# Reordering one DMA queue inside a software-pipelined attention, and the warm-up transposes ahead of it

## The chip, the cores and the metric

The kernel runs on one core of a Trainium2 chip. The metric is device time in microseconds (us); less is better. TensorE (PE) does the matmuls and the transposes, VectorE (DVE) and ScalarE (ACT) the elementwise work and the reductions, GpSimd (POOL) some more of it, and SyncE (SP) issues nearly all DMAs, one after another from one queue: what stands at its head and waits holds up all behind it.

## The reference

```python
q_n, k_n = rmsnorm(q, g_q), rmsnorm(k, g_k)          # q, k, v: 4 x 12 heads x 448 x 64, float32
scores = matmul(q_n, k_n.T) / sqrt(64)
attn = softmax(scores)                               # divided by (its row sum + 1e-9)
x = matmul(attn, v)                                  # rearranged to 1792 x 768
x = ((x @ w_a) * (x @ w_b)) @ w_out                  # 768 -> 1536 -> 768
x = (sigmoid(x @ w_gate) * (x @ w_val)) @ w_out2
```

The change concerns the attention alone.

## The kernel before

The attention works on 24 pairs of heads, one pair on the two halves of the 128 partitions. It is software-pipelined by hand. Three lists say what is emitted and in which order: `begin` (a prologue), then `turns` once for each pair (`first` is the turn of the second pair), then `end`. An entry such as `(put, -2)` calls `put` for the pair two before that of the turn. Nothing reorders the emitted instructions: the lists set the order on every engine, and that of SP's queue.

What a pair goes through, spread over several turns:

- `load`, `load_r`, `load_v`: SP loads Q, K, the remaining 64 rows, and V. The buffers are few, so each load waits for the last reader of what stood there.
- `squares`, `mean`, `rsqrt`, `newton`, `scale`: the rms normalization, the last on GpSimd. `t_tr` transposes Q and K on TensorE, `k_hi`, `k_lo`, `q_hi`, `q_lo` split each in a high and a low part.
- `s`: scores, three matmuls for each block of rows, in one of three PSUM banks (`ps_s`). `top` and `exp` take the row maximum (DVE) and the exponential with its row sum (ACT).
- `x_tr`, `x_out`: transposes of the exponentials in a unit (`unit()`, one of two two-bank PSUM tiles that all transposes share) and copies out of it. `pv`: matmuls with V, all four blocks of a pair into one PSUM bank, `pvs`, of which there is one.
- `rsum` (reciprocals of the row sums), `rsum_tr`, and `rsum_post`: ACT copies the reciprocals into a row (L453), and SP stores it to DRAM (L455). `rsum_get` (L462): SP loads that row back, once for each half of the partitions, broadcast over 64 of them each, into one of two tiles `rs`.
- `norm` (L469): DVE multiplies `pvs` by `rs`, which frees the bank for the next pair's `pv`. `put` (L475, L478): three DMAs store the result.

Two entries, `(decode, 0, 0)` and `(decode, 0, 1)`, each do a step of preparing the later layers' weights. Every few steps a block of raw weights of 384 KB is loaded by SP (L706) into a buffer that DVE has just finished reading (L724).

In the prologue `warm` issues transposes of the identity, whose results nobody reads:

```python
t = unit()
for x in range(n):
    for b in range(2):
        turned(t[:, b, 64 * (x % 6):64 * (x % 6) + 64], ident, b)
```

Of the kernel before, what the change touches and what calls it, by code (L numbers as in the profile page):

```python
# [10 lines left out]
F32 = mybir.dt.float32  # L11
# [12 lines left out]
def attention_then_two_gated_mlps(  # L24
# [37 lines left out]
    nc = tc.nc  # L62
    B, H, S, D = q.shape
    NT, DM = out.shape
    DFF = moe_w_a.shape[1]
    P = 128
# [10 lines left out]
    ident = const.tile([P, P], F32, name="ident")  # L77
# [37 lines left out]
    def attention():  # L115
# [14 lines left out]
        ps_s = sctx.enter_context(tc.tile_pool(name="ps_s", bufs=3, space=bass.MemoryType.PSUM))  # L130
# [17 lines left out]
        pvs = ps_v.tile([P, 512], F32, tag="pv", name="pv")  # L148
        nc.vector.memset(pvs, 0.0)

        def turned(out, in_, b):
            w = out.shape[-1]
            nc.tensor.transpose(out, in_[rows[b]], ident[rows[b], rows[b]])  # L153
# [53 lines left out]
        def squares(i):  # L207
            d = st[i]
            if i in (1, 2, 3):
                sq = pp.tile([P, S2], F32, tag="P", name="sq").rearrange("p (s d) -> p s d", d=D)  # L210
            else:
                sq = nr.tile([P, 14, D], F32, tag="sq" if i else "qkn", name="sq")
            r = remainder(i)
            parts = sq.rearrange("p (n s) d -> p n s d", n=2)
            if i == 0:
                nc.vector.tensor_tensor(out=parts[:, 1, 0:6], in0=d["qk"][:, 1], in1=d["qk"][:, 1], op=ALU.mult)
                nc.scalar.activation(out=parts[:, 0, 0:6], in_=d["qk"][:, 0], func=AF.Square)
                nc.scalar.activation(out=parts[:, :, 6], in_=r, func=AF.Square)
                d["sq"] = sq
                return  # L220
            if i < 3:
                nc.scalar.activation(out=parts[:, :, 0:6], in_=d["qk"], func=AF.Square)
                d["sq"] = sq
                if i > 1:
                    squares_r(i)
                return
            nc.gpsimd.tensor_tensor(out=parts[:, :, 0:6], in0=d["qk"], in1=d["qk"], op=ALU.mult)
            nc.gpsimd.tensor_tensor(out=parts[:, :, 6], in0=r, in1=r, op=ALU.mult)
            nc.gpsimd.tensor_tensor(out=sq[:, :, 0:32], in0=sq[:, :, 0:32], in1=sq[:, :, 32:64], op=ALU.add)
            d["sq"] = sq[:, :, 0:32]  # L230

        def squares_n(i, n):
            d = st[i]
            if "sq" not in d:
                d["sq"] = pp.tile([P, S2], F32, tag="P", name="sq").rearrange("p (s d) -> p s d", d=D)
            parts = d["sq"].rearrange("p (n s) d -> p n s d", n=2)
            nc.scalar.activation(out=parts[:, n, 0:6], in_=d["qk"][:, n], func=AF.Square)

        def squares_r(i):
            parts = st[i]["sq"].rearrange("p (n s) d -> p n s d", n=2)  # L240
            nc.scalar.activation(out=parts[:, :, 6], in_=remainder(i), func=AF.Square)
# [60 lines left out]
        def unit():  # L302
            return ps_tr.tile([P, 2, 512], F32, tag="tr", name="tr")
# [51 lines left out]
            for x in st[i]["K"]:  # L355
                nc.gpsimd.tensor_copy(x[64:128, 448:512], x[64:128, 0:64])

        def s(i, t):
            d = st[i]
            QH, QL = d["Q"]  # L360
            KH, KL = d["K"]
            o = P * t
            parts = [(3, slice(0, P), 64)] if t == 3 else [(t, slice(0, 64), 64), (t + 4, slice(64, P), 0)]
            ps = [ps_s.tile([P, S], F32, tag="s", name="s") for _ in parts]
            for n, (w, x) in enumerate(((QH, KH), (QL, KH), (QH, KL))):
                for (_, e, m), out_ in zip(parts, ps):
                    nc.tensor.matmul(out_, w[e, o:o + P], x[e, m:m + S], start=(n == 0), stop=(n == 2))  # L367
            for (u, *_), out_ in zip(parts, ps):
                d["ps"][u] = out_
# [154 lines left out]


        def warm(i, n):
            t = unit()
            for x in range(n):
                for b in range(2):
                    turned(t[:, b, 64 * (x % 6):64 * (x % 6) + 64], ident, b)  # L530

        begin = (
            (warm, 0, 40), (load, 0), (load_r0, 0), (load, 1), (load_g, 0), (load_r, -4), (load_r, -3), (load_r, -6),
            (load_r, -5), (load, 2), (load_r, -2), (load_r, -1), (load_v, 0), (squares, 0),
            (sums, 0, (7, 13), (0, 7), (13, 14)), (rsqrt, 0), (squares, 1), (newton, 0),
            (scale, 0, 1), (scale, 0, 2), (gain, 0), (scale, 0, 0), (load, 3), (load_r, 0), (load_v, 1), (load_r, 1),
            (t_tr, 0, 1), (k_hi, 0), (t_tr, 0, 0), (warm, 0, 16), (sums, 1, (7, 13)), (k_lo, 0), (q_hi, 0),
            (squares_r, 1), (q_lo, 0), (k_ends, 0), (sums, 1, (0, 6), (6, 14, 7)), (squares, 2),
            (s, 0, 0), (warm, 0, 12), (rsqrt, 1), (top, 0, 0), (exp, 0, 0), (newton, 1), (top, 0, 4),
            (exp, 0, 4), (s, 0, 1), (scale, 1, 1), (scale, 1, 2), (scale, 1, 0), (top, 0, 1), (exp, 0, 1), (top, 0, 5),  # L540
            (exp, 0, 5), (s, 0, 2), (t_tr, 1, 1), (s, 0, 3), (t_tr, 1, 0), (k_hi, 1), (sums, 2, (7, 14), (0, 7)),
            (top, 0, 2), (exp, 0, 2), (rsqrt, 2), (top, 0, 6), (k_lo, 1), (newton, 2), (q_hi, 1),
            (exp, 0, 6), (q_lo, 1), (k_ends, 1), (squares_n, 3, 1), (top, 0, 3), (exp, 0, 3), (squares_n, 3, 0), (squares_r, 3),
            (scale, 2, 1), (scale, 2, 0), (scale, 2, 2), (load, 4), (load_r, 2), (load_r, 3), (squares, 4),
# [6 lines left out]
            (pv, -1, 0), (scale, 2, 2), (x_out, -1, 1, 1), (top, 0, 1), (q_hi, 1), (scale, 2, 1), (exp, 0, 1), (pv, -1, 1),  # L551
            (x_tr, -1, 2), (top, 0, 5), (q_lo, 1), (x_out, -1, 2, 0), (s, 0, 2), (x_tr, -1, 3),
            (scale, 2, 0), (k_ends, 1), (mean, 3), (rsqrt, 3), (top, 0, 2), (top, 0, 6), (exp, 0, 5), (x_out, -1, 2, 1), (x_out, -1, 3),
            (s, 0, 3), (pv, -1, 2), (exp, 0, 2), (top, 0, 3), (newton, 3), (exp, 0, 6), (pv, -1, 3), (exp, 0, 3),
        )

        turns = (
            (rsum_get, -2), (early, 0), (early_hi, -1), (squares, 3), (early_lo, -1), (decode, 0, 0), (s, 0, 0), (rsum, -1), (t_tr, 1, 1),
            (top, 0, 0), (k_hi, 1), (exp, 0, 0), (x_tr, -1, 0), (top, 0, 4), (k_lo, 1), (x_out, -1, 0, 0), (s, 0, 1),
            (x_out, -1, 0, 1), (norm, -2), (mean, 3), (exp, 0, 4), (x_tr, -1, 1), (x_out, -1, 1, 0),  # L560
            (load, 4), (load_r, 3), (load_v, 1), (put, -2), (t_tr, 1, 0), (rsum_tr, -1), (rsum_post, -1),
            (pv, -1, 0), (scale, 2, 2), (x_out, -1, 1, 1), (top, 0, 1), (q_hi, 1), (scale, 2, 0), (exp, 0, 1), (pv, -1, 1),
            (x_tr, -1, 2), (top, 0, 5), (q_lo, 1), (x_out, -1, 2, 0), (rsqrt, 3), (s, 0, 2), (x_tr, -1, 3),
            (scale, 2, 1), (k_ends, 1), (top, 0, 2), (top, 0, 6), (exp, 0, 5), (x_out, -1, 2, 1), (x_out, -1, 3),
            (s, 0, 3), (pv, -1, 2), (exp, 0, 2), (top, 0, 3), (decode, 0, 1), (newton, 3), (exp, 0, 6), (pv, -1, 3), (exp, 0, 3),
        )

        end = (
            (close, -1), (rsum_get, -3), (s3, -1, fetch_third, 0), (s, -1, 0), (x_tr, -2, 0), (rsum, -2), (top, -1, 0),
            (exp, -1, 0), (x_out, -2, 0, 0), (top, -1, 4), (x_out, -2, 0, 1), (exp, -1, 4), (norm, -3), (put, -3),  # L570
            (x_tr, -2, 1), (s, -1, 1), (x_out, -2, 1, 0), (x_out, -2, 1, 1), (rsum_tr, -2), (rsum_post, -2), (top, -1, 1),
            (exp, -1, 1), (pv, -2, 0), (pv, -2, 1), (top, -1, 5), (exp, -1, 5), (x_tr, -2, 2), (s, -1, 2),
# [826 lines left out]
    with tc.manual_schedule():  # L1399
        main = mlps()  # L1400
        attention()
        open_places(6, 4, 2, 3)
        begin_mm("mm1", 3)
        for c in range(KC):
            place(where[0]["A22"], "l", c, F32, "f")
        for n, c in (("A22", 0), ("A21", 0), ("A22", 1), ("A21", 1), ("A21", 2), ("A22", 2)):
            stage_in(0, n, c)
        for c in range(KC):
            stage_in(0, "A11", c)
        low_third(1)  # L1410
        sum_third(2)
        next(main)
        cast_third(2)
        next(main)
        next(main)
        low_third(2)
        ready[0] = True
        for _ in main:
            pass
# [29 lines left out]
```

## Time and profile before

| what | value |
|---|---|
| median of 3 runs | 1227.86 us (1227.3 to 1230.31) |
| the profiled execution, time | 1234.26 us |
| the profiled execution, span from the first to the last instruction | 1232.5 us |
| TensorE busy in the span | 1176.2 us, 95% |
| VectorE busy | 924.4 us, 75% |
| ScalarE busy | 665.6 us, 54% |
| GpSimd busy | 156.3 us, 13% |
| mean granted TensorE clock | 0.974 of full speed |

The busy shares are means over a span whose first quarter (attention, up to about 303 us) and the rest (two gated layers, nearly all TensorE) have different limits. The granted clock is 1.00 at 2.4 GHz and 0.50 at 1.2 GHz. The profile and the runs are different executions, so the profiled one has its own time.

### The profile page before, as it was taken

The page shows a single profiled execution, that of the slowest core. Times are in us where ns is not written, and L with a number is a line of the kernel's source. Part 1 is how long each engine was busy: PE and PEld are TensorE (multiplying, and loading weights), DVE is VectorE, ACT ScalarE, POOL GpSimd, SP SyncE. Part 2 cuts the span into 40 slices and gives each one's busy share as a digit, 9 for nine tenths or more (in the row PEclk, how much of TensorE's full clock was granted, in tenths as well). Part 3 has the DMA queues.
Part 4 walks back from the last instruction along what each step waited for, and adds up shares of the span by engine and source line. Part 5 has one row for each costly group of instructions (what it writes and reads, how often), then busy time and mean ns, then how long its engine had stood idle before and what let it go on. Part 6 is the DMA issues. An engine that isn't in the chain of part 4 may idle for free.

```text
span 1232.5 us, 20145 instructions
## 1 busy us (share of the span) xinstructions
PE 1176.2 (95%) x7318; PEld 1014.5 (82%) x7318; DVE 924.4 (75%) x1603; ACT 665.6 (54%) x1298; POOL 156.3 (13%) x246
## 2 busy tenths in 40 slices
PE   6888888889999999999999999999999999999998
PEld 5554454555999999999999999889999999999998
DVE  6788787887876877777668679975877868667573
ACT  5777777786553444434446555644445344445542
POOL 4555547640000000000000000000000000000000
PEclk6998898899999999999999999999999999999999
DMA  5343444426623655655676664234655655687582
GB/s 132 102 127 105 123 136 127 152 72 200 236 88 120 196 170 172 203 150 162 232 274 196 201 213 144 77 105 119 186 170 172 202 151 173 211 295 241 184 270 92
DMA packets 144371, 205.90 MB, mean 167 GB/s; under 512 B 24808, under 2 KB 118160, under 8 KB 144272
## 3 DMA queue, kind: packets, MB, share of 16 engines
q1 hardware_dynamic: 143712, 204.18, 52.9%
q8 instruction: 58, 0.95, 0.3%
q10 hardware_dynamic: 432, 0.43, 0.1%
q14 instruction: 41, 0.34, 0.1%
q0 software_dynamic: 128, 0.00, 0.0%
HBM read 150.21 MB, written 54.35 MB: 166 GB/s over the span
## 4 chain that ended last, share of the span: by engine, by line
PE 82%; DVE 6%; ACT 6%; DMA 3%; issue 2%; SPq 0%; POOL 0%; DVEq 0%; ACTq 0%; POOLq 0%
PE mm L1023 48%; PE mm L1310 12%; PE mm L1320 12%; PE pv L432 5%; PE s L367 3%; ACT P L386 2%; PE tr L153 2%; ACT pt L420 2%; DMA rs<-dr 2%; DVE nm L373 1%; DVE pt L418 1%; DMA qk<-in_k_dram 1%; ACT KH L339 1%; DVE xl L651 1%; DVE d L724 0%
## 5 line engine op out<-in xcount | busy, mean ns | idle before, releaser
L1023 PE MATMUL mm<-xh,wh 128*128 128x448 f32 x1008 | 369.9, 367 | 0.7 <-ACT u L1075 0.4
L1023 PE MATMUL mm<-xh,wl 128*128 128x448 f32 x1008 | 369.2, 366 | 0.8 <-DVE wl L651 0.8
L1023 PE MATMUL mm<-xl,wh 128*128 128x448 f32 x1008 | 369.2, 366 | 0.0
L1023 PEld LDWEIGHTS mm<-xh,wh 128*128 128x128 f32 x1008 | 189.4, 188 | 20.2 <-issue 2.7
L1023 PEld LDWEIGHTS mm<-xh,wl 128*128 128x128 f32 x1008 | 189.4, 188 | 17.3 <-DVE wl L651 1.1
L1023 PEld LDWEIGHTS mm<-xl,wh 128*128 128x128 f32 x1008 | 189.5, 188 | 15.9
L651 DVE TENSOR_TENSOR wl<-d,wh 128x384 fp32r<-128x384 f32 x250 | 136.7, 554 | 65.9 <-ACT wh L1183 42.4
L837 ACT CAST wh<-d 128x384 fp32r<-128x384 f32 x166 | 81.9, 513 | 98.2 <-DVE d L825 74.6
L386 ACT ACTIVATE P<-s,nm 128x448 f32<-128x448 f32 x168 | 106.4, 641 | 34.8 <-DVE nm L373 34.7
L717 ACT ACTIVATE d<-raw 128x384 f32<-128x384 f32 x138 | 75.8, 555 | 79.5 <-DMA raw<-in_moe_w_out_dram 41.5
L724 DVE SCALAR_TENSOR_TENSOR d<-d,raw 128x384 uint32<-128x384 uint32 x138 | 77.5, 561 | 52.4 <-ACT d L717 46.8
L1183 ACT CAST wh<-d 128x384 fp32r<-128x384 f32 x84 | 43.2, 514 | 124.7 <-issue 42.7
L373 DVE TENSOR_REDUCE nm<-s 128x1 f32<-128x448 f32 x168 | 95.7, 614 | 8.6 <-PE s L367 8.0
L1320 PE MATMUL mm<-wh,gh 128*128 128x384 f32 x294 | 98.7, 336 | 0.3 <-ACT mm L1291 0.3
L1320 PE MATMUL mm<-wl,gh 128*128 128x384 f32 x294 | 98.6, 335 | 0.0
L1320 PE MATMUL mm<-wh,gl 128*128 128x384 f32 x294 | 98.5, 335 | 0.0
L1310 PE MATMUL mm<-gh,wl 128*128 128x448 f32 x252 | 92.0, 365 | 0.0
L1310 PE MATMUL mm<-gh,wh 128*128 128x448 f32 x252 | 92.0, 365 | 0.0
L1310 PE MATMUL mm<-gl,wh 128*128 128x448 f32 x252 | 92.0, 365 | 0.0
L432 PE MATMUL pv<-pt,v 128*64 128x448 f32 x288 | 78.3, 638 | 13.3 <-DVE xs L469 11.5
L367 PE MATMUL s<-KH,QH 64*128 64x448 f32 (+1 forms) x168 | 59.6, 484 | 27.8 <-ACT P L386 26.9
L720 DVE SCALAR_TENSOR_TENSOR raw<-raw 128x384 uint32<-128x384 uint32 x140 | 79.2, 566 | 4.0
(153 smaller groups left out, 1927.8 us busy)
## 6 DMA issues: line engine op xcount, KB each, us to landing
gd<-u SPq DMA_DIRECT2D x60, 448.0 KB
u<-gd SPq DMA_DIRECT2D x60, 448.0 KB
d<-wd SPq DMA_DIRECT2D x132, 192.0 KB
raw<-in_moe_w_out_dram SPq DMA_DIRECT2D x48, 384.0 KB
wd<-d SPq DMA_DIRECT2D x72, 192.0 KB
raw<-in_moe_w_a_dram SPq DMA_DIRECT2D x24, 384.0 KB
raw<-in_moe_w_b_dram SPq DMA_DIRECT2D x24, 384.0 KB
raw<-in_moe_w_val_dram SPq DMA_DIRECT2D x23, 384.0 KB
```

The lines of the kernel that those rows point to most:

```text
L367: nc.tensor.matmul(out_, w[e, o:o + P], x[e, m:m + S], start=(n == 0), stop=(n == 2))
L373: nc.vector.tensor_reduce(out=d["nm"][:, t:t + 1], in_=d["ps"][t], axis=AX.X, op=ALU.max, negate=True)
L386: nc.scalar.activation(out=e, in_=d["ps"].pop(t), func=AF.Exp, bias=d["nm"][:, t:t + 1], accum_out=d["sum"][:, t:t + 1])
L432: nc.tensor.matmul(pvs[64 * h:64 * h + 64, o:o + S], w, x, start=(n == 0), stop=(n == R), skip_group_check=True)
L651: eng.tensor_tensor(out=lo, in0=t, in1=f32(hi), op=ALU.subtract)
L717: nc.scalar.activation(out=f32(t), in_=f32(high), func=AF.Copy, scale=2.0 ** -112)
L720: nc.vector.scalar_tensor_tensor(out=low, in0=high, scalar=0x80000000, in1=low, op0=ALU.bitwise_and, op1=ALU.bitwise_or)
L724: nc.vector.scalar_tensor_tensor(out=t, in0=t, scalar=3, in1=low, op0=ALU.logical_shift_left, op1=ALU.bitwise_or)
L837: nc.scalar.copy(out=hi, in_=t)
L1023: nc.tensor.matmul(ps[:, o:o + S], w[:, P * c:P * c + P], x[:, x0:x0 + S], start=(p in (1, 5) and c == 0 and z == 0), stop=(c == KC - 1 an ...
L1310: nc.tensor.matmul(ps[:, o:o + S], w[:, P * un:P * un + P], g[:, g0:g0 + S], start=(p in (1, 5) and f == 0 and z == 0), stop=(f == HF - 1 ...
L1320: nc.tensor.matmul(ps[:, o:o + HB], g[:, P * t:P * t + P], w, start=(p in (1, 5) and f == 0 and z == 0), stop=(f == HF - 1 and z == 2), sk ...
```

## The change

Four edits. (1) In a turn, the load of the reciprocals, `rsum_get`, goes from the head of the turn after (for the pair two before) to a place behind the last scores of the turn before (for the pair one before), ahead of the second decode step; `first` gets it too, and `end` loses one. (2) `put` moves behind `rsum_post`. (3) `warm` transposes the whole 128x128 identity into `pvs`, in place of two halves into a unit, and there are other counts of it at other places: 26, 4, 6, 12 and 6 in place of 40, 16 and 12 pairs. (4) In the prologue the second block of scores of the first pair goes right behind the first, into a unit of the transposes.

```diff
-        def s(i, t):
+        def s(i, t, pair=False):
...
-            ps = [ps_s.tile([P, S], F32, tag="s", name="s") for _ in parts]
+            if pair:
+                both = unit()
+                ps = [both[:, b, 0:S] for b in range(2)]
+            else:
+                ps = [ps_s.tile([P, S], F32, tag="s", name="s") for _ in parts]
...
         def warm(i, n):
-            t = unit()
             for x in range(n):
-                for b in range(2):
-                    turned(t[:, b, 64 * (x % 6):64 * (x % 6) + 64], ident, b)
+                o = 64 + P * (x % 3)
+                nc.tensor.transpose(pvs[:, o:o + P], ident, ident)
...
-            (warm, 0, 40), (load, 0), (load_r0, 0), (load, 1), (load_g, 0), (load_r, -4), (load_r, -3), (load_r, -6),
+            (warm, 0, 26), (load, 0), (load_r0, 0), (load, 1), (load_g, 0), (load_r, -4), (load_r, -3), (load_r, -6),
...
-            (t_tr, 0, 1), (k_hi, 0), (t_tr, 0, 0), (warm, 0, 16), (sums, 1, (7, 13)), (k_lo, 0), (q_hi, 0),
+            (t_tr, 0, 1), (warm, 0, 4), (k_hi, 0), (t_tr, 0, 0), (warm, 0, 6), (sums, 1, (7, 13)), (k_lo, 0), (q_hi, 0),
...
-            (s, 0, 0), (warm, 0, 12), (rsqrt, 1), (top, 0, 0), (exp, 0, 0), (newton, 1), (top, 0, 4),
-            (exp, 0, 4), (s, 0, 1), (scale, 1, 1), (scale, 1, 2), (scale, 1, 0), (top, 0, 1), (exp, 0, 1), (top, 0, 5),
-            (exp, 0, 5), (s, 0, 2), (t_tr, 1, 1), (s, 0, 3), (t_tr, 1, 0), (k_hi, 1), (sums, 2, (7, 14), (0, 7)),
+            (s, 0, 0), (s, 0, 1, True), (warm, 0, 12), (rsqrt, 1), (top, 0, 0), (exp, 0, 0), (newton, 1), (top, 0, 4),
+            (exp, 0, 4), (scale, 1, 1), (scale, 1, 2), (scale, 1, 0), (top, 0, 1), (exp, 0, 1), (top, 0, 5),
+            (exp, 0, 5), (s, 0, 2), (t_tr, 1, 1), (s, 0, 3), (t_tr, 1, 0), (warm, 0, 6), (k_hi, 1), (sums, 2, (7, 14), (0, 7)),
...
         turns = (
-            (rsum_get, -2), (early, 0), (early_hi, -1), (squares, 3), (early_lo, -1), (decode, 0, 0), (s, 0, 0), (rsum, -1), (t_tr, 1, 1),
+            (early, 0), (early_hi, -1), (squares, 3), (early_lo, -1), (decode, 0, 0), (s, 0, 0), (rsum, -1), (t_tr, 1, 1),
...
-            (load, 4), (load_r, 3), (load_v, 1), (put, -2), (t_tr, 1, 0), (rsum_tr, -1), (rsum_post, -1),
+            (load, 4), (load_r, 3), (load_v, 1), (t_tr, 1, 0), (rsum_tr, -1), (rsum_post, -1), (put, -2),
...
-            (s, 0, 3), (pv, -1, 2), (exp, 0, 2), (top, 0, 3), (decode, 0, 1), (newton, 3), (exp, 0, 6), (pv, -1, 3), (exp, 0, 3),
+            (s, 0, 3), (rsum_get, -1), (pv, -1, 2), (exp, 0, 2), (top, 0, 3), (decode, 0, 1), (newton, 3), (exp, 0, 6), (pv, -1, 3), (exp, 0, 3),
```

What this moves in SP's queue is seen in a turn that has a raw load: here around the stores of the fifth pair's result (`xd_0_4_87`), with the row's store (`dr`), the loads of the reciprocals (`rs_287`) and the raw weights:

```order
-L475 DMA xd_0_4_87<-xs 128x384
-L478 DMA xd_0_4_87<-xs 64x64 x2
-L455 DMA dr<-row 7x128
-L706 DMA raw<-in_moe_w_b_dram 128x3x256
-L462 DMA rs_287<-dr 64x448 x2
+L459 DMA dr<-row 7x128
+L479 DMA xd_0_4_87<-xs 128x384
+L482 DMA xd_0_4_87<-xs 64x64 x2
+L466 DMA rs_287<-dr 64x448 x2
+L709 DMA raw<-in_moe_w_b_dram 128x3x256
```

The row's store now comes first, and the loads of `rs` stand ahead of the raw load instead of behind it; in turns without a raw load only the row's store and put change places.

On TensorE, the prologue from the first pair's transposes of K on; in brackets stand the engines whose semaphores an instruction waits for. Before:

```order
L153 MATMUL tr<-ident,qkn 128x64 [waits DVE_49] x2
L153 MATMUL tr<-ident,qkn 128x64 x6
L153 MATMUL tr<-ident,qkn 128x64 [waits PE_49]
L153 MATMUL tr<-ident,qkn 128x64 x5
L153 MATMUL tr<-ident,qrem 128x64 x2
L153 MATMUL tr<-ident 128x64 [waits DVE_49,Activation_49]
L153 MATMUL tr<-ident 128x64 x31
L367 MATMUL s<-KH,QH 128x448 [waits Activation_49]
L367 MATMUL s<-KH,QH 128x448
L367 MATMUL s<-KH,QL 128x448 [waits DVE_49]
L367 MATMUL s<-KH,QL 128x448
L367 MATMUL s<-KL,QH 128x448 x2
```

And of the change, from behind the transposes of K on:

```order
L533 MATMUL pv<-ident 128x128 x4
L153 MATMUL tr<-ident,qkn 128x64 x6
L153 MATMUL tr<-ident,qrem 128x64 x2
L533 MATMUL pv<-ident 128x128 x6
L371 MATMUL s<-KH,QH 128x448 [waits Activation_49]
L371 MATMUL s<-KH,QH 128x448
L371 MATMUL s<-KH,QL 128x448 [waits DVE_49]
L371 MATMUL s<-KH,QL 128x448
L371 MATMUL s<-KL,QH 128x448 x2
L371 MATMUL tr<-KH,QH 128x448 [waits PE_49]
L371 MATMUL tr<-KH,QH 128x448
L371 MATMUL tr<-KH,QL 128x448 x2
```

The warm-up transposes behind those of Q no longer wait for VectorE and ScalarE, and the second block of scores (here `tr<-KH,QH`, since it lies in a unit) follows the first without waiting for an exponential.

## Rows read from the trace of the kernel before

**Rows 1.** The page, part 2: busy tenths and granted clock in 40 slices.

```profile
...
PE   6888888889999999999999999999999999999998
...
PEclk6998898899999999999999999999999999999999
...
```

**Rows 2.** Waits of VectorE, 40 to 310 us: total us, times, longest us.

```profile
...
DVE xs L469 <- issue: 7.3, 4, 2.9
...
DVE xs L469 <- DMA qk<-in_k_dram: 4.2, 2, 2.2
DVE xs L469 <- DMA rs<-dr: 3.7, 2, 2.0
...
```

**Rows 3.** Waits of TensorE, 40 to 310 us, the same columns.

```profile
...
PE pv L432 <- DVE xs L469: 11.5, 8, 2.5
...
```

**Rows 4.** Chain of waits, 88 to 106 us: start, length, what.

```profile
...
97.13 4.53 DMA qk<-in_k_dram
...
```

**Rows 5.** Timeline of SP's queue: start, length (us), line, what it issues.

```profile
...
60.84 0.43 SPq L455 DMA_DIRECT2D dr<-row  x1
62.21 1.10 SPq L462 DMA_DIRECT2D rs<-dr  x2
...
90.74 0.43 SPq L455 DMA_DIRECT2D dr<-row  x1
95.44 0.39 SPq L706 DMA_DIRECT2D raw<-in_moe_w_b_dram  x1
95.92 1.11 SPq L462 DMA_DIRECT2D rs<-dr  x2
...
```

**Rows 6.** Timeline, norm (VectorE) and row copy (ScalarE); idle before in brackets.

```profile
...
65.93 0.69 DVE L469 TENSOR_TENSOR xs<-pv,rs 128x512 f32<-128x512 f32 x1 [0.69 <-issue]
88.44 0.68 DVE L469 TENSOR_TENSOR xs<-pv,rs 128x512 f32<-128x512 f32 x1
...
90.04 0.25 ACT L453 COPY row<-tr 7x128 f32<-7x128 f32 x1
...
101.73 0.69 DVE L469 TENSOR_TENSOR xs<-pv,rs 128x512 f32<-128x512 f32 x1 [2.18 <-DMA qk<-in_k_dram]
...
```

**Rows 7.** Stretches: length, busy PE, PEld, DVE, ACT, POOL, clock, DMA share, GB/s.

```profile
65.93:233.68 167.75, 140.86 (x1457) 83.14 (x1455) 134.70 (x288) 126.12 (x348) 97.68 (x144) 0.90 0.43 124
233.68:263.96 30.28, 27.53 (x317) 16.58 (x317) 27.73 (x61) 27.32 (x76) 20.71 (x30) 1.00 0.38 117
...
101.73:113.34 11.61, 10.09 (x78) 5.47 (x80) 9.09 (x22) 6.72 (x19) 5.28 (x8) 0.74 0.38 114
...
sum 46.09, PE 39.70 PEld 21.75 DVE 36.08 ACT 28.35 POOL 23.56; mean PE 9.92 PEld 5.44 DVE 9.02 ACT 7.09 POOL 5.89
...
173.59:183.15 9.56, 7.80 (x78) 4.42 (x80) 8.99 (x21) 6.56 (x19) 5.44 (x8) 1.00 0.61 183
sum 19.10, PE 15.61 PEld 8.83 DVE 17.96 ACT 13.14 POOL 10.88; mean PE 7.80 PEld 4.41 DVE 8.98 ACT 6.57 POOL 5.44
```

**Rows 8.** TensorE's groups (busy us, mean ns), 2-5.2 us, then 5.52-5.9.

```profile
L153 PE MATMUL tr<-ident 64*128 64x64 f32 x65 | 3.7, 312 | 0.0
...
L153 PE MATMUL tr<-ident 64*128 64x64 f32 x12 | 0.7, 256 | 0.0
```

**Rows 9.** Timeline of the prologue on TensorE, and QL on VectorE.

```profile
...
10.06 1.01 PE L153 MATMUL tr<-ident,qkn 64*128 64x64 f32 x13 [0.88 <-DVE qkn L284]
...
12.53 1.97 PE L153 MATMUL tr<-ident 64*128 64x64 f32 x32 [1.35 <-DVE KL L350]
14.23 0.75 PE L367 MATMUL s<-KH,QH 64*128 64x448 f32 x2
...
12.30 0.68 DVE L334 TENSOR_TENSOR QL<-tr,QH 128x512 fp32r<-128x512 f32 x1
...
```

**Rows 10.** Busy time by stretch, columns as in rows 7.

```profile
19.20:36.10 16.90, 13.98 (x94) 8.87 (x95) 11.39 (x25) 10.67 (x30) 10.35 (x19) 0.50 0.30 82
36.20:66.90 30.70, 25.89 (x309) 16.33 (x309) 26.02 (x56) 24.88 (x71) 16.35 (x26) 1.00 0.41 122
```

More of the change, by code (lines that the diff above doesn't have):

```diff
@@ L553, in attention @@
             (scale, 2, 0), (k_ends, 1), (mean, 3), (rsqrt, 3), (top, 0, 2), (top, 0, 6), (exp, 0, 5), (x_out, -1, 2, 1), (x_out, -1, 3),
-            (s, 0, 3), (pv, -1, 2), (exp, 0, 2), (top, 0, 3), (newton, 3), (exp, 0, 6), (pv, -1, 3), (exp, 0, 3),
+            (s, 0, 3), (rsum_get, -1), (pv, -1, 2), (exp, 0, 2), (top, 0, 3), (newton, 3), (exp, 0, 6), (pv, -1, 3), (exp, 0, 3),
         )
         turns = (
-            (rsum_get, -2), (early, 0), (early_hi, -1), (squares, 3), (early_lo, -1), (decode, 0, 0), (s, 0, 0), (rsum, -1), (t_tr, 1, 1),
+            (early, 0), (early_hi, -1), (squares, 3), (early_lo, -1), (decode, 0, 0), (s, 0, 0), (rsum, -1), (t_tr, 1, 1),
             (top, 0, 0), (k_hi, 1), (exp, 0, 0), (x_tr, -1, 0), (top, 0, 4), (k_lo, 1), (x_out, -1, 0, 0), (s, 0, 1),
             (x_out, -1, 0, 1), (norm, -2), (mean, 3), (exp, 0, 4), (x_tr, -1, 1), (x_out, -1, 1, 0),
-            (load, 4), (load_r, 3), (load_v, 1), (put, -2), (t_tr, 1, 0), (rsum_tr, -1), (rsum_post, -1),
+            (load, 4), (load_r, 3), (load_v, 1), (t_tr, 1, 0), (rsum_tr, -1), (rsum_post, -1), (put, -2),
             (pv, -1, 0), (scale, 2, 2), (x_out, -1, 1, 1), (top, 0, 1), (q_hi, 1), (scale, 2, 0), (exp, 0, 1), (pv, -1, 1),
@@ L564, in attention @@
             (scale, 2, 1), (k_ends, 1), (top, 0, 2), (top, 0, 6), (exp, 0, 5), (x_out, -1, 2, 1), (x_out, -1, 3),
-            (s, 0, 3), (pv, -1, 2), (exp, 0, 2), (top, 0, 3), (decode, 0, 1), (newton, 3), (exp, 0, 6), (pv, -1, 3), (exp, 0, 3),
+            (s, 0, 3), (rsum_get, -1), (pv, -1, 2), (exp, 0, 2), (top, 0, 3), (decode, 0, 1), (newton, 3), (exp, 0, 6), (pv, -1, 3), (exp, 0, 3),
         )
         end = (
-            (close, -1), (rsum_get, -3), (s3, -1, fetch_third, 0), (s, -1, 0), (x_tr, -2, 0), (rsum, -2), (top, -1, 0),
+            (close, -1), (s3, -1, fetch_third, 0), (s, -1, 0), (x_tr, -2, 0), (rsum, -2), (top, -1, 0),
             (exp, -1, 0), (x_out, -2, 0, 0), (top, -1, 4), (x_out, -2, 0, 1), (exp, -1, 4), (norm, -3), (put, -3),
```

## Prediction

> **What bounds the kernel now.** I read the page first. In 40 slices of 31 us TensorE shows a 9 nearly everywhere; an 8 or less stands only in the first nine and in the last, and the same nine hold every lowered digit of the granted clock [rows 1]. So time is to be found in the first 300 us, the attention, and the change touches nothing else. Next I asked who waits there. On VectorE one line stands out: L469 (norm), which multiplies the PV bank by the broadcast reciprocals `rs`, waited 7.3 + 4.2 + 3.7 = 15.2 us in 8 turns [rows 2]. TensorE waited 11.5 us, 8 times, for norm itself, since pv needs the bank that norm must read first [rows 3].
>
> Then the chain of waits around one such turn: 4.53 us of it pass until a DMA has landed, and norm follows [rows 4]. The profile calls that DMA qk<-in_k_dram, which norm does not read; it is the last one to land by the profile, and I read it as the landing of `rs`, issued 1.2 us before it. SP's own rows say the same [rows 5]: the store of the row (L455) left at 90.74, and SP stood until 95.44, because the next thing in its queue was a raw weight load (L706), whose buffer VectorE had not finished reading. `rs` left behind it at 95.92, and norm started at 101.73, 2.18 us after VectorE was free [rows 6], that is, it could have run at 99.55.
>
> The third view is a table of stretches from one norm to the next [rows 7]. 14 turns from 65.93 to 233.68 take 167.75 us, 12.0 each, with VectorE busy 134.70, 9.62 each. Three turns without a wait (233.68 to 263.96) take 30.28, 10.1 each, with VectorE busy 27.73, 9.24 each, at a granted clock of 1.00. Raw loads come every second turn, so long and short stretches alternate. The stretch behind a late norm holds the same 78 matmuls each time, yet two of them take 19.10 us together at clock 1.00 (9.55 each), and four at 0.72 to 0.84 take 46.09 (11.52 each). A late norm thus costs twice: the wait, and in some turns a fall from 2.4 to 1.2 GHz behind it.
>
> **The change part by part.** *SP's order in a turn.* The loads of `rs` move from the head of the following turn to a place ahead of the second decode step, so they pass the raw load. The stores of put (three DMAs) move behind the store of the row. No DMA is added or dropped. In the turn of rows 5 the new order gives: ScalarE has the row at 90.29 [rows 6], so L455 goes at about 90.3; put is released by then (norm ended at 89.12) and fills the time in which the row lands, 1.5 us of issuing; `rs` goes at about 92.3. I check that against the gap from L455 to L462 where nothing stands between: 60.84 to 62.21, 1.37 us. So `rs` leaves about 3.6 us earlier, against a wait of 2.18. From the issue of `rs` to norm the trace has 5.81 us with a raw load just ahead (95.92 to 101.73) and 3.72 without (62.21 to 65.93; norm waited 0.69 there, so this is a true landing) [rows 5, 6]. From 92.3 it lands between 96.0 and 98.1, ahead of 99.55: the wait goes, with 1.4 to 3.5 us to spare.
>
> When turns shrink, so does the slack. The row is ready 1.85 us after norm (88.44 to 90.29), `rs` then leaves at norm + 3.9 and lands at norm + 7.6 to 9.7, in turns of 10.1 to 10.5. It still fits, barely at the far end; that is a rival below.
>
> What is queued behind the moved pieces: behind `rs`, which waits for the row's landing, stands the raw load, and that waits for VectorE until 95.4 anyway, 2 us after `rs` is out. Behind it stand the loads of the next turn, as now. put now waits for the row copy, about 1.5 us more; what it stores is read many turns later, and its buffer is wanted two turns later. I cost all this at nothing. If the 2 us of cover went, the raw load and its decode would be late by what is lacking. In turns where norm was on time, an earlier `rs` buys nothing. In the end list the third-last pair's `rs` only moves up.
>
> The gain of this part, bounded twice. By waits: 15.2 us at VectorE, or 11.5 at TensorE if the rest was hidden, and for the clock 46.09 - 4 x 9.55 = 7.9 if all of it comes back, nothing if the clock falls as often as now. That is 11.5 to 23.1. By work: VectorE's 9.62 a turn and the 0.85 that it idles in turns without a wait (10.09 - 9.24) make 10.47, times 14 is 146.6 against 167.75, 21.1 us. The second is near the top of the first. I take 19, since other waits that lie beside this one will show when it goes.
>
> *The prologue.* The first warm-up is now 26 whole transposes in place of 80 half ones. The trace shows no 128x128 transpose of float32. From below, its time goes with the columns: 65 half ones took 3.7 us, 57 ns each [rows 8], so 114 for twice the columns and 3.0 us in all. From above, none overlaps the next, at 312 ns each from start to end: 8.1 us. Started in the first 2 us, as the eighty are now, they end between 5 and 10, ahead of the thirteen transposes at 10.06 that wait for VectorE [rows 9]: hidden either way, and I take the lower end, for matmuls overlap everywhere else.
>
> The second warm-up costs something now: its 32 transposes waited until 12.53 for KL, because they took the transposes' next unit, and the first scores came behind them at 14.23, though QL, the last of their operands, was there at 12.98 [rows 9]. In the PV bank the new 4 + 6 wait for nothing: 1.1 us at 114 ns each, 3.1 at 312, from about 10.8 on, with Q's transposes between. The scores then start by 12.4 instead of 14.23, 1.8 us earlier; their third matmul needs QL and, at the pace of the first two (0.75 us from start to end), would ask for it near 12.9, so 0.1 is lost again. With the upper price they start at 13.9, 0.3 earlier. The second scores, which take a unit and no longer wait for the first exponential, come right behind. I count 1.7 us, passed on by top, exponential, newton and GpSimd's scaling into the first turn. Bounds: 0, if the upper price holds and the clock behind the warm-ups is lower than now, to 4.6, if besides the stretch 19.2 to 36.1, now wholly at 0.50 [rows 10], comes to full clock (16.9 - 16.9 / 1.21 = 2.9, by the ratio 11.52 / 9.55).
>
> Here a rule speaks against the warm-ups. The row first: of the first 80 transposes those up to 5.2 us took 312 ns each, the last ones 256 on average [rows 8]; they quickened while nothing but transposes had run. The Trainium skill (TensorE: Matmul & The Clock Gate, Part 4) says that the full clock does not engage for transposes, which do not count as busy in the same way. By it the warm-ups buy no clock, and the prologue's gain lies between 0 and 1.7; by the row, up to 4.6. The trace disagrees with the rule, and 1.7 stands in both.
>
> **Sum.** 19 + 1.7 = 20.7, rounded to 21. The profiled execution took 1234.26 us (span 1232.5 and 1.8 around it) and would take 1213; the median of the runs is 1227.86, 6.4 below it. I take the same difference from the median: **1207 us**.
>
> **Rivals.**
> 1. *The row's round trip stays too long.* put's three DMAs, now between row and `rs`, slow the landing, and shorter turns eat the slack (norm + 9.7 against 10.1). For: 5.81 was measured. Against: the raw load that stood ahead then is behind now. If half of every wait stays and no clock comes back, 7.6 + 1.7 = 9.3, 1218.5.
> 2. *The wait was hidden anyway.* VectorE and ScalarE take the time as other waits. For: VectorE was busy 134.70 of 167.75 us. Against: the three quiet turns at 10.1. Only the prologue stays, 1226, within 0.3%.
> 3. *Slower: the prologue stays cold.* The clock now stands at 1.00 over the 30.7 us from 36.2 [rows 10]. If the new prologue makes it miss that rise, they take 1.21 times as long, 6.4 us more. This decides only where SP's order gives less than 2.7 (6.4 - 3.7): 1234 with rival 2's condition, but 1215 beside the 19. Against: the rise came out of a busy stretch at half clock (13.98 of 16.90), whose matmuls the change keeps.
> 4. *More.* Both bounds met, 23.1 + 4.6: 1200.
>
> **How the numbers follow.** The forecast has 0.60 (1203 to 1213 by itself), rival 1 0.20, rival 2 0.10, rival 3 ending slower 0.04, rival 4 0.06. The range 1199 to 1220 holds the forecast and rivals 1 and 4 less their tails, and leaves no more than 2 in 10 outside. About 0.3%, 3.7 us, is what a measurement of this kernel can tell from no change. Faster by more: 0.60 + 0.20 + 0.06 = 0.86; rival 2 counts as same, 0.10; slower 0.04.
>
> **What would show it.** Right: SP issues `rs` some 2 us after the row's store in every turn, never behind a raw load; norm's wait on DMAs falls from 15.2 us to under 3; turns from 66 us on last 10.1 to 10.7; the clock is above 0.95 over them (0.90 now [rows 7]); the first scores start near 12.4. Wrong: norm still waits 1 to 2 us in odd turns (rival 1), or waits no more and the turns still last 12 (rival 2), or the clock rows show 0.50 long past 36 us (rival 3). The rest of the kernel should take the same time as now, only earlier; if it grows, weights are late there, and the prediction falls short by what it grows.

## The result, and the profile after

| | before | after |
|---|---|---|
| median of 4 runs each, same chip | 1229.09 us (1227.30 to 1232.12) | 1212.99 us (1210.93 to 1213.84) |
| profiled execution, span | 1234.26, 1232.5 | 1213.13, 1211.4 |
| first norm, last norm, from there to the end | 44.4, 303.5, 929.0 | 42.5, 283.5, 927.8 |

The ratio is 0.9864, with a 95% interval of 0.9839 to 0.9889: 16.1 us faster, where 21 was forecast. Between the two profiled executions the difference is 21.1.

The page of after, its first part and two lines of the second (40 slices of 30.3 us), which answer to [rows 1]:

```profile
PE 1164.7 (96%) x7236; PEld 1009.4 (83%) x7236; DVE 930.9 (77%) x1603; ACT 666.5 (55%) x1298; POOL 157.3 (13%) x246
...
PE   6888888999999999999999999999999999999998
...
PEclk8999999999999999999999999999999999999999
```

The clock digits that stood at 6 and 8 in the first 300 us are gone, but for the very first slice. TensorE's 8s remain there: it still waits in the attention, only not for this.

The instructions of norm (L473 now) in after: duration, then what its engine sat idle for until it could start.

```profile
L473 DVE TENSOR_TENSOR xs<-pv,rs x24: 675/678/692, 42.5 to 283.5; 128x512 f32<-128x512 f32 x24
its engine sat idle before it (us, times) until:
  PE pv L436: 0.5, 1
```

No DMA is left in that list; in before it held 15.2 us [rows 2]. SP's queue in after shows why, in the turn that answers to the second half of [rows 5] (start, length, line, what it issues):

```profile
85.77 0.29 SPq L459 DMA_DIRECT2D dr<-row  x1
86.15 0.36 SPq L479 DMA_DIRECT2D xd<-xs  x1
86.57 1.11 SPq L482 DMA_DIRECT2D xd<-xs  x2
87.78 1.72 SPq L466 DMA_DIRECT2D rs<-dr  x2
90.90 0.38 SPq L709 DMA_DIRECT2D raw<-in_moe_w_b_dram  x1
```

`rs` is issued 2.0 us after the row's store, with put between them, and SP then stands until 90.90 for the raw load's buffer, with nothing urgent behind it. Norm of this turn starts at 94.94, 7.2 us after the issue.

Stretches from norm to norm in after, the same turns as in [rows 7] (columns: span; busy time of PE, PEld, DVE, ACT, POOL; clock, DMA share, GB/s):

```profile
63.30:214.68 151.38, 132.50 (x1472) 79.26 (x1470) 141.36 (x289) 126.97 (x350) 98.79 (x144) 0.97 0.47 135
214.68:244.87 30.19, 27.45 (x317) 16.58 (x315) 27.71 (x61) 27.23 (x76) 20.58 (x30) 1.00 0.40 124
```

The 14 turns went from 167.75 to 151.38 us, 10.81 each, and the clock from 0.90 to 0.97. The three turns that never waited take what they took (30.28, now 30.19). So the 21.1 us of the profile add up: first norm 1.9 earlier, 18.1 between the first and the last norm, 16.4 of it in these 14 turns, and 1.1 behind. One number speaks against a clean win: VectorE is busy 141.36 us in the 14 turns instead of 134.70, with the same work. Nor are the 14 turns alike. Ten of them last 10.48 us on average, the other four more:

```profile
94.94:106.68 11.74, 10.49 (x109) 6.91 (x106) 10.13 (x23) 9.24 (x26) 6.30 (x10) 0.86 0.46 122
117.45:128.69 11.24, 10.31 (x107) 5.74 (x105) 9.45 (x23) 8.67 (x25) 6.30 (x10) 0.85 0.42 118
191.10:203.49 12.39, 9.30 (x109) 5.66 (x107) 11.86 (x21) 9.51 (x27) 8.54 (x12) 1.00 0.43 127
203.49:214.68 11.19, 10.43 (x107) 6.10 (x105) 9.52 (x22) 9.40 (x26) 7.99 (x11) 0.85 0.36 98
```

In three of them the granted clock fell to 0.50 for 3.4 us. In the one from 191.10, at 1.00 throughout, VectorE is busy for 11.86 us: an instruction of 0.16 us (L443, of `rsum`) took 2.07 there. Experiments 6 and 12 come to that.

TensorE in the first 18 us of after, which answers to [rows 9]:

```profile
1.59 5.15 PE L533 MATMUL pv<-ident 128*128 128x128 f32 x26 [1.59 <-POOL ident masks.py:199]
...
10.66 1.11 PE L533 MATMUL pv<-ident 128*128 128x128 f32 x4
...
12.33 1.54 PE L533 MATMUL pv<-ident 128*128 128x128 f32 x6
13.80 0.74 PE L371 MATMUL s<-KH,QH 64*128 64x448 f32 x2
...
16.30 1.53 PE L533 MATMUL pv<-ident 128*128 128x128 f32 x12
```

A whole transpose takes 0.20 us in the row of 26, and 0.26 to 0.28 in the rows of 4 and 6, not the 0.114 that I took. The granted clock makes the difference: the six at 12.33 run at 0.50, and the twelve at 16.30, at 1.00, take no longer than they do. The ten of the second warm-up fill 2.65 us of TensorE, and the first scores start at 13.80 (before 14.23), not at 12.4.

### The profile page after: what moved, and what is told of

It is laid out like the page before. It is cut to its first block, busy times and chain, and to the rows that moved or that the text cites. A ratio compares the mean times of both kernels' runs of the same rounds, so it can differ in the third digit from the quotient of the medians.

```text
span 1211.4 us, 19984 instructions
## 1 busy us (share of the span) xinstructions
PE 1164.7 (96%) x7236; PEld 1009.4 (83%) x7236; DVE 930.9 (77%) x1603; ACT 666.5 (55%) x1298; POOL 157.3 (13%) x246
## 4 chain that ended last, share of the span: by engine, by line
PE 82%; DVE 8%; ACT 7%; issue 1%; DMA 1%; POOL 1%; SPq 0%; DVEq 0%; ACTq 0%; POOLq 0%
PE mm L1026 49%; PE mm L1313 13%; PE mm L1323 12%; PE pv L436 4%; ACT P L390 3%; PE s L371 3%; DVE nm L377 2%; ACT pt L424 2%; PE tr L153 2%; DVE pt L422 1%; DVE y L275 1%; DVE xl L654 1%; ACT KH L339 1%; DVE d L727 0%; DMA qk<-in_q_dram 0%
## 5 line engine op out<-in xcount | busy, mean ns | idle before, releaser
L720 ACT ACTIVATE d<-raw 128x384 f32<-128x384 f32 x138 | 75.9, 555 | 74.9 <-DMA raw<-in_moe_w_out_dram 42.3
L371 PE MATMUL s<-KH,QH 64*128 64x448 f32 (+1 forms) x166 | 55.9, 461 | 29.4 <-ACT P L390 29.1
L723 DVE SCALAR_TENSOR_TENSOR raw<-raw 128x384 uint32<-128x384 uint32 x140 | 79.1, 565 | 4.0
L436 PE MATMUL pv<-pt,v 128*64 128x448 f32 x288 | 73.4, 596 | 2.0 <-DVE pt L422 0.6
```

The lines of the kernel that those rows point to most:

```text
L436: nc.tensor.matmul(pvs[64 * h:64 * h + 64, o:o + S], w, x, start=(n == 0), stop=(n == R), skip_group_check=True)
L720: nc.scalar.activation(out=f32(t), in_=f32(high), func=AF.Copy, scale=2.0 ** -112)
L723: nc.vector.scalar_tensor_tensor(out=low, in0=high, scalar=0x80000000, in1=low, op0=ALU.bitwise_and, op1=ALU.bitwise_or)
```

## The experiments

My theory: norm waited because `rs` stood behind a raw load that was itself waiting; passing it is the whole gain, and the prologue adds a little. Its rivals: put's move does it, the prologue does it, or any order that sends `rs` elsewhere does. Each kernel was timed in five rounds beside before; ratios are to its median on the same chip, with 95% intervals. These medians were 1231.11 us (experiments 1, 2, 5, 6), 1229.94 (3, 4, 7, 9) and 1229.96 (8, 10, 11, 12), so that times of different groups compare only to within some 2 us.

**1. SP's order alone.** The lists of the turns as in after, the prologue as in before:

```diff
-            (warm, 0, 26), (load, 0), ...
+            (warm, 0, 40), (load, 0), ...
```

> The lists of the turns and of the end as changed (rsum_get ahead of the second decode step, put behind rsum_post), the prologue of the kernel before. If the gain is norm's wait for the reciprocals, nearly all of it is here: 12 to 15 us less than before, norm never idle for a DMA, turns of 10.1 to 10.8 us. If the prologue carries half of the gain (rival: its clock), 7 to 9 us less.

Measured: 1213.86 us, ratio 0.9858 (0.9835 to 0.9881). Norm waits for no DMA, and the 14 turns take 10.75 us each. The gain of after (0.9864) is here without its prologue.

**2. The prologue alone,** on the lists of before, once here and once more on another chip (experiment 8):

```diff
-            (s, 0, 3), (rsum_get, -1), (pv, -1, 2), ...
+            (s, 0, 3), (pv, -1, 2), ...
...
+            (rsum_get, -2), (early, 0), ...
```

> The prologue as changed (warm-ups in the bank of PV, second scores in a unit), the lists of the turns and of the end as before. Theory: 1 to 3 us less than before, and norm waits for the reciprocals in the odd turns as before, some 15 us in all. Rival (half of the gain is the prologue's): 7 to 9 us less.

Measured: 1224.75 us, 0.9954 (0.9934 to 0.9975). Norm waits 14.3 us as before.

**3. The loads of `rs` alone,** on before (`first` and `end` as in after):

```diff
-            (rsum_get, -2), (early, 0), ...
+            (early, 0), ...
...
-            (s, 0, 3), (pv, -1, 2), ...
+            (s, 0, 3), (rsum_get, -1), (pv, -1, 2), ...
```

> The kernel before with one edit: the load of the reciprocals moved ahead of the second decode step, put and the prologue as before. By the theory this alone is the gain of the queue: 13 to 17 us less than before, and norm waits under 3 us in all. By the rival, that the row's store had to get ahead of put as well, since put waits for norm and the row behind it, norm still waits 5 us or more and the gain is 6 to 10 us.

Measured: 1214.12 us, 0.9871 (0.9846 to 0.9895); norm's waits come to 0.98 us in two turns. This one entry is nearly the whole change.

**4. put alone,** on before:

```diff
-            (load, 4), (load_r, 3), (load_v, 1), (put, -2), (t_tr, 1, 0), (rsum_tr, -1), (rsum_post, -1),
+            (load, 4), (load_r, 3), (load_v, 1), (t_tr, 1, 0), (rsum_tr, -1), (rsum_post, -1), (put, -2),
```

> The kernel before with one edit: put behind the store of the row, the load of the reciprocals still at the head of the next turn, behind the raw load. Theory: nothing, within 3 us of before, and norm waits some 15 us as before. Rival (the row's earlier store is what counts): 6 us less or more.

Measured: 1229.62 us, 1.000 (0.9982 to 1.0018), norm's waits 15.3 us. put's place buys nothing by itself, and between row and `rs` it costs nothing that experiments 1 and 3 could tell.

**5. `rs` behind the raw load again,** one place later in SP's queue; all else as in after:

```diff
-            (s, 0, 3), (rsum_get, -1), (pv, -1, 2), (exp, 0, 2), (top, 0, 3), (decode, 0, 1), (newton, 3), ...
+            (s, 0, 3), (pv, -1, 2), (exp, 0, 2), (top, 0, 3), (decode, 0, 1), (rsum_get, -1), (newton, 3), ...
```

> The changed kernel, but with the load of the reciprocals one entry later, behind the second decode step of the same turn, so that it follows the raw weight load again in SP's queue; in the turns without a raw load nothing changes. If standing behind the raw load is the whole cause, norm waits again in the odd turns, 12 to 15 us in all, and the time is 10 to 14 us above that of the changed kernel, within 3 us of before less the prologue's share. If instead the row's earlier store (put behind rsum_post) or the earlier place in the turn is what counts, it stays within 4 us of the changed kernel.

Measured: 1227.73 us, 0.9975 (0.9958 to 0.9992), 14.7 above after and 13.9 above experiment 1. SP's queue of this kernel in the turn shown for after:

```profile
89.90 0.29 SPq L459 DMA_DIRECT2D dr<-row  x1
...
95.03 0.38 SPq L709 DMA_DIRECT2D raw<-in_moe_w_b_dram  x1
95.51 1.10 SPq L466 DMA_DIRECT2D rs<-dr  x2
```

and its waits of VectorE from 40 to 310 us (total, times, longest):

```profile
DVE xs L473 <- DMA rs<-dr: 5.9, 3, 2.4
DVE xs L473 <- DMA qk<-in_q_dram: 4.3, 2, 2.4
...
DVE xs L473 <- issue: 2.5, 1, 2.5
DVE xs L473 <- DMA qk<-in_k_dram: 1.8, 1, 1.8
```

With put in its new place and the new prologue, but `rs` behind the raw load, it leaves 5.6 us after the row's store instead of 2.0, and the 14.5 us of waits are back, under the same mixed names as in [rows 2]. So the place behind the raw load is the cause; that these names all stood for `rs` is now shown too, since they came and went with it.

**6. What may have taken back part of it.** In after VectorE had 6.7 us more in the 14 turns. The rows that grew most are those of newton, which works on tiles of 128x14: 6.0 us more (a decode instruction, L721, has 1.9 more). VectorE in one turn of after, and under it GpSimd in the same stretch:

```profile
70.54 1.01 DVE L275 SCALAR_TENSOR_TENSOR y<-t,y 128x14 f32<-128x14 f32 x1
```

```profile
70.35 1.18 POOL L229 TENSOR_TENSOR sq<-sq 128x448 f32<-128x448 f32 x1
```

L275 normally takes 0.17 us; here it ends within 0.02 us of GpSimd's addition L229. In before 6 of the 24 were held so, in after 10; beyond 0.175 us each, newton's three instructions cost 7.8 us in before and 13.7 in after, over all 24 pairs. The Trainium skill (SBUF — State Buffer, SBUF: two separate sides) says that VectorE and GpSimd have one pair of SBUF ports in common, and that of a VectorE instruction with two inputs in SBUF and a GpSimd instruction that reads SBUF the one that starts first has the pair to its end, while the other stands. The trace agrees for L275, which reads two tiles and starts 0.19 us after L229: 1.01 us against 0.17.

The experiment moves newton to behind `k_lo` of the following turn, when GpSimd has nothing to do (so `first` loses its second newton), and leaves all else of after:

```diff
-            (s, 0, 3), (rsum_get, -1), (pv, -1, 2), (exp, 0, 2), (top, 0, 3), (decode, 0, 1), (newton, 3), (exp, 0, 6), ...
+            (s, 0, 3), (rsum_get, -1), (pv, -1, 2), (exp, 0, 2), (top, 0, 3), (decode, 0, 1), (exp, 0, 6), ...
...
-            ... (top, 0, 4), (k_lo, 1), (x_out, -1, 0, 0), (s, 0, 1),
+            ... (top, 0, 4), (k_lo, 1), (newton, 2), (x_out, -1, 0, 0), (s, 0, 1),
```

> The changed kernel with newton (three instructions of VectorE on 128x14) moved from the end of a turn to behind k_lo of the next one, where GpSimd waits for a transpose. In the changed kernel these three take 13.7 us more than their shortest time in all, most of it where the third (L275) ends together with GpSimd's addition of squares (L229); in the kernel before it was 7.7. If this overlap is a wait on VectorE that the change uncovered, and VectorE sets the turn, the time falls by 6 to 12 us below the changed kernel, L275 taking 0.18 us everywhere. If the time beside it is slack, it stays the same within 2 us; if scale then waits for newton, it rises.

Measured: 1206.97 us (1204.51 to 1207.58), 0.9805 (0.9782 to 0.9829): 6.0 less than after, 6.9 less than experiment 1. L275 over the whole kernel, after first and then this one (durations in ns: least, median, most):

```profile
L275 DVE SCALAR_TENSOR_TENSOR y<-t,y x24: 173/176/1021, 7.1 to 241.5; 128x14 f32<-128x14 f32 x24
```

```profile
L275 DVE SCALAR_TENSOR_TENSOR y<-t,y x24: 173/174/176, 7.2 to 238.1; 128x14 f32<-128x14 f32 x24
```

and the 14 turns of this kernel, with the columns as above:

```profile
62.00:207.50 145.50, 129.71 (x1488) 77.64 (x1484) 137.09 (x289) 125.96 (x351) 99.60 (x144) 1.00 0.50 144
```

151.38 became 145.50, 10.39 a turn, with VectorE at 137.09, and the clock stays at 1.00: in this profile it does not fall once between 32 us and the last 4 us of the kernel.

That newton's holds alone cost these 6 us is not shown, and turn by turn the rows speak against it. The ten turns of after that last 10.48 lose 0.7 us together, though newton is held for about 1 us in nine of them. Nearly all the rest is in the four long turns: 2.5 us in the first two, and 2.8 in the last two, the first of which has in after the hold of L443, beside GpSimd's subtraction L505:

```profile
199.47 2.07 DVE L443 TENSOR_SCALAR rc<-sum 128x7 f32<-128x7 f32 x1
```

```profile
199.43 2.07 POOL L505 TENSOR_TENSOR xl<-xst,xh 128x896 fp32r<-128x896 f32 x1 [0.30 <-ACT xh L499]
```

With newton out of its way L443 ends at 194.39 in that turn, and L505 starts at 194.49. Experiments 1 and 9, which differ in newton's place alone, say the same: 4.0 of the 5.1 us between their 14 turns lie in these two turns. Nor did the holds vanish. VectorE's time fell by 4.3 us in the 14 turns, not by the 10.8 that newton's holds did, since L443 now meets L229 in eight turns (up to 1.08 us, 3.1 more in all) and a decode instruction, L723, takes 3.2 more. So the move is worth 6 us, and it met its forecast in part by luck. No run keeps newton where it was and takes L443 from L505, and none has newton moved without these other holds.

The next wait shows itself too: the reciprocals' first instruction (L443) now waits 12.5 us for the last exponential, in after 4.2.

**7. No warm-ups at all,** after without any of its warm-up transposes, whose results nobody reads:

```diff
-            (warm, 0, 26), (load, 0), ...
+            (load, 0), ...
```

> The changed kernel with all its warm-up transposes left out (no output depends on them). If the warm-ups lift the clock in the prologue, the granted clock stays at 0.50 longer up to 36 us, the first norm comes 1 us or more later than at 42.5, and the time is 1 to 4 us above that of the changed kernel. If they only take time (10 of them stand ahead of the first scores for 2.6 us), the first scores start near 12.4 instead of 13.8 and the time is 0 to 2 us below.

Measured: 1211.37 us, 0.9847 (0.9821 to 0.9872), 1.6 below after, with intervals that overlap. The first scores start at 11.51 us, 2.3 earlier than in after, and the first norm at 41.6 instead of 42.5, although TensorE seems to run at half speed up to 32.9 us. (This profile's records of the clock begin there, with the rise to 1.00; ahead of it the pace speaks: two matmuls of the scores take 0.57 us at 13.08, as in after at 0.50, where at 1.00 they take 0.37.) In after the clock stood at 1.00 from 6.0 to 9.4 and from 16.2 to 26.4. The warm-ups stood in front of the first scores, and in these two profiles that cost more than they bought. Of the 2.3 us only 0.9 are left at the first norm; what took the rest no run shows.

**8. The prologue alone, again,** the kernel of experiment 2:

> The new prologue alone on the kernel before, once more. It gained 5.7 us there, but nothing beside the new queue order. If that gain is real, it comes again (4 to 7 us less than before); if it lay in how often the granted clock happened to fall, 0 to 3 us.

Measured: 1227.61 us, 0.9984 (0.9967 to 1.0). In experiment 2 the distance was 6.4 us, here 2.4. The two profiles of this one kernel have spans of 1221.9 and 1231.7: the clock is at 0.50 for 20.5 us between 66 and 303 us in the one, for 34 in the other, and the waits of norm are 14.3 and 15.8. What decides how often it falls behind a late norm is not settled.

**9. Newton moved, old prologue:** experiment 6 with the prologue of before (its edit is that of experiment 1).

> The changed kernel's turns with newton moved to the next turn (as in the run before), but with the prologue of the kernel before. In that run the granted clock did not fall again after the prologue, so what the new prologue is worth by itself shows here against it: 1 to 3 us by the forecast, so 1208 to 1210 here against 1207. If the 5.7 us that the new prologue gained alone on the kernel before come from the prologue itself, 1212 to 1214.

Measured: 1206.78 us (1206.53 to 1207.38), 0.981 (0.9787 to 0.9834), level with experiment 6 and better than I expected. With these turns the new prologue is worth nothing that can be measured.

**10. Newton moved, on before:** the edit of experiment 6 with SP's order untouched.

> The kernel before with newton moved to the next turn alone. There newton's three instructions take 7.8 us more than their shortest time, in the odd turns, ahead of a norm that waits for the reciprocals anyway. If norm's wait covers them, 0 to 3 us less than before; if VectorE's work counts there too, 6 us less or more, as it did behind the change.

Measured: 1227.67 us, 0.9982 (0.9967 to 0.9996). Newton's excess fell to 0.9 us here as well, yet the kernel gained 2.3, not 6, and norm still waits 15.0 us. VectorE's waits of this kernel, 40 to 310 us:

```profile
DVE xs L469 <- DMA rs<-dr: 5.3, 3, 1.9
...
DVE xs L469 <- DMA qk<-in_q_dram: 5.0, 3, 1.8
DVE xs L469 <- DMA xst<-xd: 2.6, 1, 2.6
...
DVE xs L469 <- DMA qk<-in_k_dram: 2.1, 2, 1.7
```

I expected that norm's wait for `rs` covers newton's holds here, and the small gain fits that, but it isn't shown. Holds on L439 (the L443 of after) came in their place, 3.4 us more in the 14 turns. And the turn in which L439 met GpSimd's subtraction in before and the one behind it (12.54 and 12.38 us) last 10.47 and 10.77 here, 3.7 less, while the other twelve are 0.5 longer together.

**11. Newton moved and no warm-ups:** experiments 6 and 7 together.

> The changed kernel with newton moved to the next turn and all warm-up transposes left out (no output depends on them). The one gave 6 us, the other 0 to 2: 1204 to 1207 if they add.

Measured: 1205.57 us (1204.93 to 1206.62), 0.9799 (0.9783 to 0.9815). The lowest of all, 24.4 us below before and 7.4 below after, but only 1.4 below experiment 6, less than times of different groups can tell.

**12. The reciprocals later as well:** experiment 11 with `rsum` behind the first `top`, to take away the wait of L443 for the exponential.

```diff
-            (early, 0), ... (s, 0, 0), (rsum, -1), (t_tr, 1, 1),
-            (top, 0, 0), (k_hi, 1), ...
+            (early, 0), ... (s, 0, 0), (t_tr, 1, 1),
+            (top, 0, 0), (rsum, -1), (k_hi, 1), ...
```

> As the kernel beside it (newton moved, no warm-ups), and the reciprocals of the row sums (rsum) behind the first maximum of the turn instead of ahead of it. With newton moved, VectorE waits 12.5 us in 15 turns there for the last exponential of the pair before. If that wait sets the turn, 4 to 10 us less than the kernel beside it; if TensorE and ScalarE bound the turn by now (PE busy 9.2 of 10.4 us), the same within 2 us.

Measured: 1221.84 us, 0.9928 (0.9911 to 0.9945): a miss, 16.3 above experiment 11. L443's wait did fall, from 15.1 to 1.9 us, and the turns up to 166 us last 10.3. But six turns from there to 243 us last 12 to 13.3. VectorE in one of them, and GpSimd beside it:

```profile
200.77 1.87 DVE L443 TENSOR_SCALAR rc<-sum 128x7 f32<-128x7 f32 x1
```

```profile
200.53 2.09 POOL L505 TENSOR_TENSOR xl<-xst,xh 128x896 fp32r<-128x896 f32 x1 [1.91 <-ACT xh L499]
```

In exactly these six turns L443, 0.16 us by its median, takes 1.66 to 1.87 beside GpSimd's subtraction L505, and ends with it. In after it met that subtraction in one turn (2.07 us at 199.47), which lasted 12.4; so it did in before (2.07 at 217.28). TensorE's waits of this kernel from 166 to 243 us show what hangs on it:

```profile
PE tr L153 <- DVE t L273: 8.4, 6, 1.5
```

Its next transposes wait for VectorE six times, once for each hold, and behind five of them the clock falls to 0.50 for 3.4 us. A hold of 1.5 to 1.7 us thus became 2.4 us a turn (12.8 against 10.4).

## Why the prediction was right, and where its terms were off

**`rs` passes the raw load: right.** In the turn shown it is issued 2.0 us behind the row's store, as worked out (2.0 to 3.1 in the turns from 44 to 257 us), and never behind a raw load. Experiments 3 and 5 show that it is this place and nothing else: with it 1214, without it 1228.

**Norm's wait goes: right,** 15.2 us to none. Rival 1, a round trip too long, did not come: from the issue of `rs` to norm 7.2 us pass in the turn shown, and norm was not waiting for it. **put costs nothing: right** (experiments 3 and 4).

**The wait was not hidden anyway (rival 2).** It fell with 14.7 us between after and experiment 5.

**The turns: close, and the missing part lies in four of them.** I forecast 10.1 to 10.7 us; they last 10.81. The bound by work gave 10.47, and ten of the 14 turns last 10.48 on average. The other four hold 4.6 us more: 1.9 in the turn in which L443 is held, 2.7 in the three in which the clock fell. I allowed 2 us for waits that lie beside this one. The bound also took VectorE's 9.62 us a turn as fixed, and it became 10.10, mostly by newton, which met GpSimd in 10 turns instead of 6; but experiment 6 doesn't show that this made the turns longer. The clock over the turns is 0.97, as forecast above 0.95.

**The prologue: price wrong, and of little use.** Whole transposes cost 0.20 to 0.28 us, nearer to the upper bound (0.312) than to the lower that I took. The lower one came from half transposes, which start two at a time in the trace of before, a pair every 0.107 us; the whole ones of after start one at a time, every 0.213 us until 5.9 us and every 0.109 from 6.0 on, when the clock is at 1.00. The ten ahead of the scores ran at 0.50. So the scores started at 13.80, not 12.4. Over the profiles, the first norm starts at 43.8 us on average with the old prologue (six kernels, 42.8 to 44.9), at 42.7 with the new (five, 41.5 to 44.1), at 42.0 with no warm-ups (three, 41.6 to 42.3): 1.1 us for the change, in place of 1.7, and another 0.7 for leaving the warm-ups out, both less than the profiles with warm-ups differ among themselves. By the ratios it is nothing where norm waits no more (0.9858 without it against 0.9864 with it; 0.981 against 0.9805 in experiments 9 and 6), and 2.4 to 6.4 us where norm still waits (8 and 2) and the runs spread most. The clock did rise in the first warm-up (1.00 from 5.96 us, with nothing but transposes ahead of it), as the rows had it and against the rule that was weighed there. But it bought no time: the prologue is no longer without the warm-ups.

**Rival 3, a cold prologue: not so.** The clock is back at 1.00 for a long stretch from 33.3 us, before from 36.2; even with no warm-up it gets there by 32.9 (experiment 7).

**The rest unchanged: right,** 928.98 and 927.83 us from the last norm to the end, within what the profiles of all kernels show (926.9 to 929.0).

**The step that was off** is the last one, the step from the profile to the median, and behind it two terms of the sum. The sum of 21 was made against the profiled execution (1234.26) and met it: 21.1. That is partly luck, since 1.1 of it lies behind the last norm, where I expected nothing. I then took the same difference from the median, 6.4 us lower, and got 1207, where 1213 came. At the medians the turns alone gave 17.3 us (experiment 1) where I took 19, and the prologue beside them nothing that can be measured where I took 1.7. (The other 1.2 of the 6 us is the median of before itself, 1229.09 with its fourth run.)

I read the difference between profile and medians so: an execution of before that takes long does so largely by what the change removes, late norms and the falls of the clock behind them, so the gain at the median is smaller than at such an execution. For it speaks that one kernel with late norms has spans 9.8 us apart in which these two differ (experiment 8). The clock noted for each run bears out a part. In each of the three sets of before the longer runs are those with the lower mean clock (correlation -0.64 to -0.86; 0.55 to 0.63 us for each 0.001). The profiled execution had 0.974, the median of each set is 0.979: by these numbers, an estimate, some 3 of the 6.4 us go with the clock. What the rest is no run shows. Against the medians the sum is 5 us too large.

## What to carry to other kernels

Look in an in-order DMA queue for a small load on the critical path behind a big one that waits for its buffer; passing it costs one line, and putting it back behind the big one is the test. When a wait goes, look next at small VectorE instructions beside a long one of GpSimd: here some of 0.16 us lasted as long as that one did. The length of a hold is not its price: one of 1.5 to 1.7 us on L443 came to 2.4 a turn (experiment 12), while ten turns without newton's holds of 1 us, though with shorter ones on L443, were 0.7 us shorter together (experiment 6). So compare the turns one by one before you name the cause of a gain: a move can undo a hold that it wasn't made for. And if a profiled execution stands well above the median, take from the median only what its own turns would lose.

## What was not expected of the hardware

- A VectorE instruction on 128x7 or 128x14 elements, 0.16 to 0.17 us long, takes up to 2.07 us beside one of GpSimd, and ends with it. Six such holds of L443 in experiment 12 go with 16 us; nine turns of after with one on newton's L275 or L273, about 1 us each, are hardly longer than those of experiment 6. L275 reads two tiles in SBUF, as in the rule cited in experiment 6; L443 reads one, and why it is held too no run here shows.
- Late waits and the clock add up. TensorE in the turns of experiment 6 keeps 1.00 throughout, with VectorE's share of those turns at 137.09 of 145.50 us; with one late wait of 2 us every second turn, in before, it is 0.90. But in after the clock fell three times in these turns (at 94.7, 118.6 and 203.9 us) with no late norm, and why it fell the first two times no run shows.
- The spread of the runs did not go with norm's wait alone. The standard deviation is 2.1 to 2.4 us in the three sets of before and 0.4 to 1.4 in experiments 6, 9 and 11, but 2.0 in experiment 1 and 2.3 in experiment 3, where norm hardly waits either (4 or 5 runs each).
